# Attention tails packed into quarter and half arrays, and a ninth group of tokens by seven products

## The chip, the cores and the metric

The kernel runs on one core of a Trainium2 chip. A core has five engines with queues of their own: TensorE (PE in the profile), VectorE (DVE), ScalarE (ACT), GpSimd (POOL) and SyncE (SP). TensorE multiplies on an array of 128 rows by 128 columns and writes to eight PSUM banks; VectorE and ScalarE read these banks; GpSimd and SyncE here mostly start DMA transfers. The metric is the device time of one execution in microseconds (us), lower is better.

## What is computed

Attention with a bias by distance, for 8 batches, 8 heads, 576 positions and a head size of 64, followed by a feed-forward layer over the 4608 tokens. Cut to what matters:

```python
scores = scale * np.matmul(q, k.transpose(0, 1, 3, 2))       # [8, 8, 576, 576], scale = 1/8
bias = bias_table[bucket]                                    # bucket by |i - j|, 32 buckets
scores = scores + bias.transpose(2, 0, 1)[None]
attn = exp(scores - max);  attn = attn / (attn.sum(-1) + 1e-9)
x = np.matmul(attn, v)                                       # -> [4608, 512]
h = x @ w_in                                                 # [4608, 2048]
s = np.sin(alpha * h)
g = h + s * s / (alpha + 1e-09)
out = g @ w_out                                              # [4608, 512], float32
```

576 is 4 * 128 + 64: every batch has a last 64 keys and a last 64 queries that fill only half of an array. "Tails" below are these.

## The kernel before, in words

**Attention.** Heads go in four pairs p. A score tile (`qk_t`, task T) is 128 keys by 256 queries for both heads of a pair; the two heads of 64 dimensions lie in the upper and the lower 64 rows of the array ("rows" mode). Two such key chunks make one PSUM tile of 1024 columns, which ScalarE turns to `u` by one Exp (`exp_u`), and VectorE multiplies by exp(bias) where the bias is not constant (`band_t`). The tails have tasks of their own: L0 and L1 (`qk_tail`, last keys against the first 512 queries, two pairs each), R0 and R1 (`qk_r`, the first 512 keys against the last queries) and S (`qk_s`, last keys against last queries). For L and S the batches from the third on use `kd`, in which `corners` (VectorE) puts the last keys of both heads on a block diagonal: one matmul of the full array gives both heads. The first two batches use 64x64 tiles, one per head ("quad" mode).

**Values.** `av_w` (tasks av) multiplies `u` by v. It takes 128 queries as the stationary operand, and per pair it issues one matmul of 130 columns for the last keys and eight of 65 columns for the other keys (64 values and a column of ones for the sum). For w=0 it covers two chunks of 128 queries, for w=1 two chunks and the last 64 queries, which stand as a third chunk of 128 with the other half unused. `norm` (VectorE) divides, and `turn_x` (a DMA transpose, SP) or `turn_x_pe` (TensorE and a copy, batch 0) turns the result to `xT`. The tokens stand in the order of the output, 576 for each batch.

**Feed-forward.** The tokens go in blocks of 512, the last two of 448 and 576. For each block and each of 16 slices f of the hidden width, `moe_in` issues four matmuls against w_in, ScalarE does Sin (`moe_sin`), ScalarE or VectorE squares (`moe_sq`), VectorE forms g (`moe_g`). Groups of 512 tokens of g are multiplied by w_out. Groups 0 to 7 go by seven products of 256x256 blocks instead of eight (`moe_fast`, `products`): VectorE forms sums of g (`gate_sum`, four in two halves per group) and of w_out (`weight_sum`, once), and joins the products to quarters of the output (`quarter`, `quarter_sum`). Group 8 goes directly (`moe_out`, `moe_half`). Some products run as two at a time in halves of 64 rows ("rows" mode, listed in `OPT["rows"]`).

**The order.** `_graph` makes tasks with an engine, dependencies and rings of buffers; `_Plan.run` puts them in order; here the order of each engine is given outright by `LINE`. Each engine then works its queue strictly in that order. GpSimd's queue starts with `clear` (zeros in `us` and `kd`) and then issues the loads. `OPT["scalar"]` lists the tasks that ScalarE takes instead of VectorE.

The functions that the change touches, and what calls them:

Of the kernel before, what the change touches and what calls it, by code (L numbers as in the profile page):

```python
# [9 lines left out]
F16 = mybir.dt.float16  # L10
# [6 lines left out]
NP = H // 2  # L17
NF = FF // 128
XR = 4 * S
# [338 lines left out]
def _line(text):  # L358

    out, i = [], 0  # L360
    for x in text.split():
# [71 lines left out]


COLD = dict(turn_half=(0.22, 0.38), turn=(0.4, 0.48), qkT=(0.22, 0.42), qkR=(0.23, 0.43),
            qkL=(0.43, 0.62), qkS=(0.12, 0.24), turn_x=(0.2, 0.27))


def _graph(K, opt):
# [1265 lines left out]
```

## Time and profile before

| | before |
|---|---|
| median of 3 runs, us | 373.93 (372.23 to 373.96) |
| profiled execution, us from the first to the last instruction | 370.6 |
| TensorE matmul busy, us | 356.4 (96%), 4379 matmuls |
| VectorE busy, us | 318.8 (86%) |
| ScalarE busy, us | 318.4 (86%) |
| GpSimd busy, us | 87.9 (24%) |
| granted TensorE clock | 1.000 |

The page has no other time of the profiled execution than this span. A busy TensorE in the profile need not be at its peak: matmuls overlap, and one of 512 columns is shown with 379 ns, while four of them follow each other within 0.86 us. Where the rate matters, the view to read is the chain of work that ended last: each of its pieces shows how long a number of matmuls held the chain. An "idle before" that is named with an engine is time that the engine waited for it.

### The profile page before, as it was taken

How to read it: one execution, taken by the hardware profiler on the slowest of the kernel's cores; microseconds unless marked ns; L12 is line 12 of the kernel's file. 1: busy time of each engine (PE TensorE's matmuls, PEld its weight loads, DVE VectorE, ACT ScalarE, POOL GpSimd, SP SyncE). 2: the span in 40 equal slices, each digit the busy share in tenths (PEclk: the TensorE clock that was granted, in tenths of full speed). 3: DMA queues.
4: the chain of work that ended last, by engine and by line, in shares of the span. 5: the costliest groups of instructions: out<-in, count | busy, mean ns of one | idle time of the engine just before them, and what ended most of it. 6: DMA issues, size and time to landing. Idle time of an engine off the chain costs nothing.

```text
span 370.6 us, 10525 instructions
## 1 busy us (share of the span) xinstructions
PE 356.4 (96%) x4379; PEld 245.9 (66%) x4379; DVE 318.8 (86%) x711; ACT 318.4 (86%) x424; POOL 87.9 (24%) x105
## 2 busy tenths in 40 slices
PE   4969999999999999999999999999999999999996
PEld 3647546764666569755788987666965766745675
DVE  2679999999989998989998998899879997989733
ACT  5897999999999999999998999999899798476310
POOL 8895523085108000820050006200000000000000
PEclk9999999999999999999999999999999999999999
DMA  8999999899949954999799039907230012220014
GB/s 161 224 154 180 206 171 156 104 134 157 182 83 135 142 127 75 156 155 88 125 210 95 18 84 142 157 3 155 79 48 2 10 47 79 56 85 2 0 58 170
DMA packets 152415, 40.86 MB, mean 110 GB/s; under 512 B 134432, under 2 KB 151920, under 8 KB 152368
## 3 DMA queue, kind: packets, MB, share of 16 engines
q0 software_dynamic: 96656, 18.45, 60.2%
q1 hardware_dynamic: 55008, 21.22, 28.0%
q8 instruction: 34, 0.56, 0.6%
q10 hardware_dynamic: 704, 0.53, 0.6%
q14 instruction: 13, 0.11, 0.1%
HBM read 36.94 MB, written 15.93 MB: 143 GB/s over the span
## 4 chain that ended last, share of the span: by engine, by line
PE 87%; ACT 4%; POOL 3%; DMA 2%; DVE 2%; issue 1%; ACTq 0%; POOLq 0%; DVEq 0%
PE acc L1514 32%; PE acc L1611 26%; PE acc L1461 10%; PE acc L1405 9%; PE acc L1451 3%; PE acc L1558 3%; DMA wt<-in_k_dram 2%; PE acc L1364 2%; ACT s L1522 1%; PE acc L1395 1%; POOL mt L1292 1%; PE acc L1632 1%; DVE g L1543 1%; ACT u L1413 1%; POOL v L1219 1%
## 5 line engine op out<-in xcount | busy, mean ns | idle before, releaser
L1514 PE MATMUL acc<-xT,w_in 128*128 128x512 f16 (+3 forms) x704 | 134.2, 340 | 0.7 <-DVE g L1543 0.4
L1413 ACT ACTIVATE u<-acc 128x1024 f16<-128x1024 f32 x128 | 124.3, 1035 | 8.4 <-PE acc L1405 6.4
L1543 DVE SCALAR_TENSOR_TENSOR g<-s,inv_a,acc 128x512 f16<-128x512 f16 (+2 forms) x160 | 104.5, 691 | 8.6 <-ACT s L1527 6.5
L1522 ACT ACTIVATE s<-acc,alphaT 128x512 f16<-128x512 f32 (+2 forms) x144 | 93.2, 684 | 14.7 <-PE acc L1514 10.6
L1514 PEld LDWEIGHTS <-w_in 128*128 128x128 f16 x704 | 64.4, 98 | 55.8 <-DVE g L1543 1.8
L1611 PEld LDWEIGHTS <-g 128*128 128x128 f16 (+1 forms) x768 | 59.8, 96 | 18.0 <-issue 4.4
L1441 DVE TENSOR_TENSOR u<-u,toep 128x256 f16<-128x256 f16 (+1 forms) x128 | 59.4, 487 | 1.8 <-DMA toep<-e_sb 0.9
L1219 POOL DMA_DIRECT2D v<-in_v_dram x32 | 36.8, 1278 | 99.3 <-PE acc L1461 93.3
L1611 PE MATMUL acc<-w_out,g 128*128 128x256 f16 (+1 forms) x496 | 54.1, 271 | 0.0
L1405 PE MATMUL acc<-qT,kT 64*128 64x256 f16 x512 | 46.3, 279 | 3.9 <-DVE qT L1350 1.9
L1461 PE MATMUL acc<-v,u 128*128 128x65 f16 x1024 | 45.0, 193 | 0.1
L1527 ACT ACTIVATE s<-s 128x512 f16<-128x512 f16 (+2 forms) x67 | 41.4, 629 | 1.5
L1461 PEld LDWEIGHTS <-u 128*128 128x128 f16 x1024 | 40.6, 97 | 1.4 <-issue 0.5
L1611 PE MATMUL acc<-wt,g 128*128 128x256 f16 (+1 forms) x272 | 38.4, 272 | 0.0
L1611 PE MATMUL acc<-wt,sums 128*128 128x256 f16 (+1 forms) x272 | 34.6, 273 | 0.0
L1529 DVE TENSOR_TENSOR s<-s 128x512 f16<-128x512 f16 (+2 forms) x77 | 31.9, 422 | 2.6 <-ACT s L1522 2.3
L1472 DVE TENSOR_TENSOR xp<-acc,rden 128x256 f16<-128x256 f32 (+1 forms) x64 | 31.4, 491 | 2.2
L1405 PEld LDWEIGHTS <-kT 64*128 64x128 f16 x512 | 20.3, 96 | 16.1 <-issue 12.2
L1611 PEld LDWEIGHTS <-sums 128*128 128x128 f16 (+1 forms) x272 | 23.5, 97 | 7.9 <-issue 2.5
L1451 PE MATMUL acc<-vt,ut 128*128 128x130 f16 x128 | 28.3, 221 | 0.1
L1225 POOL DMA_DIRECT2D vt<-in_v_dram x16 | 14.1, 894 | 33.6 <-PE acc L1461 30.6
L1492 DVE COPY quarter<-acc 128x512 f32<-128x512 f32 x18 | 12.4, 687 | 9.3 <-PE acc L1611 4.7
(90 smaller groups left out, 361.6 us busy)
## 6 DMA issues: line engine op xcount, KB each, us to landing
out_dram<-quarter SPq DMA_DIRECT2D x32, 256.0 KB, 2.7
v<-in_v_dram POOLq DMA_DIRECT2D x32, 128.0 KB, 8.7
staged_k<-in_k_dram POOLq DMA_DIRECT2D x6, 576.0 KB, 10.8
staged_q<-in_q_dram POOLq DMA_DIRECT2D x5, 576.0 KB, 9.9
w_out<-in_moe_w_out_dram POOLq DMA_DIRECT2D x4, 512.0 KB, 8.7
w_in<-in_moe_w_in_dram POOLq DMA_DIRECT2D x4, 512.0 KB, 16.2
sums<-in_q_dram POOLq DMA_DIRECT2D x7, 144.0 KB, 5.6
out_dram<-outs SPq DMA_DIRECT2D x3, 256.0 KB, 2.0
```

The lines of the kernel that those rows point to most:

```text
L1219: self.nc.gpsimd.dma_start(out=self.vs[t % 2][:, c, :, 0:D], in_=src)
L1405: self.nc.tensor.matmul(out=s[:, o:o + 256], lhsT=self.kT[t % 2][r, p, 128 * c:128 * c + 128], rhs=self.qT[t % 2][r, p, 256 * w:256 * w + ...
L1413: self.nc.scalar.activation(out=c["u"], in_=c["s"], func=AF.Exp, scale=0.125)
L1441: self.nc.vector.tensor_tensor(out=io, in0=io, in1=m, op=ALU.mult)
L1451: nc.tensor.matmul(out=c["av"][:, 130 * j:130 * j + 130], lhsT=tail, rhs=vt[:, p, :], start=True, stop=True, skip_group_check=True)
L1461: nc.tensor.matmul(out=c["av"][:, 130 * j + 65 * a:130 * j + 65 * a + 65], lhsT=l, rhs=vv[:, ch, 2 * p + a, 0:65], start=False, stop=True, ...
L1514: self.nc.tensor.matmul(out=c["h"][:, x:y], lhsT=self.w_in[:, j, 128 * f:128 * f + 128], rhs=self.xT[:, j, at:at + y - x], start=(j == 0 a ...
L1522: self.nc.scalar.activation(out=c["s"], in_=c["h"], func=AF.Sin, scale=self.alphaT[:, f:f + 1])
L1527: self.nc.scalar.activation(out=c["s"], in_=c["s"], func=AF.Square)
L1529: self.nc.vector.tensor_tensor(out=c["s"], in0=c["s"], in1=c["s"], op=ALU.mult)
L1543: self.nc.vector.scalar_tensor_tensor(out=o, in0=c["s"][:, x:y], scalar=self.inv_a[:, f:f + 1], in1=c["h"][:, x:y], op0=ALU.mult, op1=ALU.add)
L1611: self.nc.tensor.matmul(out=c[to][:, 256 * k:256 * k + 256], lhsT=a[r, 128 * k:128 * k + 128], rhs=b[r, :], start=to not in c["began"], st ...
```

## The change

- **Last keys (L, S).** `kd` and `corners` go. `tail` issues four 64x64 matmuls for two pairs at once, into the four quarters of the array, in all batches. The heads that stand in the upper and lower half of the result alternate from pair to pair, and `mask`, `load_vt` (four smaller loads for each batch instead of two) and `memsets` follow that.
- **Last queries (values).** `av_w` covers two chunks for w=0 and w=1 alike. A new `av_tails` does the last queries of all four pairs in a batch: 64 queries are the stationary operand, and two pairs go to the two column halves of the array ("cols" mode). `norm_tails` and `turn_tails` (for batch 0 `turn_tails_pe`) bring them to a tile `xt`.
- **Groups.** A group is now the first 512 tokens of one batch, and the last 64 tokens of all eight batches are a ninth group. All nine blocks have 512 tokens and all nine groups go by seven products; the order of the groups is 0 to 6, the tails, 7. The last group ends by `ending`: its last product in two halves of 256 columns that are copied and stored one by one. `store` and its like write to the rows that belong to the group.
- **Start.** `clear` goes. The loads are in a new order.
- **Order and shares.** `LINE`, the products in rows mode, the list of ScalarE's tasks (51 squares instead of 67) and the number of `u` buffers (14 instead of 12) are new.

```diff
 LINE = """
-0 2 5 1 12 1 390 -21 229 -232 6 17 -112 324 -303 130 -137 154 134 17 -287 497 -265 268 -156 20 -37
...
+82 -68 66 8 2 -73 192 -125 43 7 3 -39 -12 18 20 -28 17 -35 112 -80 83 -99 -2 15 -6 102 -4 -36 42 -55
...
-    add("POOL", 2.05, E("clear"), seq="GQ")
...
-        T_v[t] += [gq(0.65, "load_vt", (t, a), deps=pre, pipe=0.27) for a in range(2)]
+        T_v[t] += [gq(0.6, "load_vt", (t, a, b), deps=pre, pipe=0.14) for a in range(2) for b in range(2)]
...
-            if not kind:
-                e = add("DVE", 0.42, E("corners", t, range(NP)), deps=[c], prio=0.3)
...
         ct = cells[t, ("L", p // 2)]
-        cr, cs = (cells[t, ("R", p // 2)], cells[t, ("S",)]) if w else (None, None)
-        need = tiles + [ct] + ([cr, cs] if w else [])
+        need = tiles + [ct]
...
+    def close_tails(t):
+
+        need = [cells[t, ("R", 0)], cells[t, ("R", 1)], cells[t, ("S",)]]
+        acell, xcell, users, xu = {}, {}, [], []
+        av = add("PE", 0.66, None, deps=[c["done"] for c in need] + T_v[t],
+                 prio=opt["p_av"], take=[(1, users)], mode="cols", name=f"avt{t}")
+        av.emit = lambda: K.av_tails(acell, tag(av), need[:2], t)
...
+            T_t[t] = add("SP", 1.2, lambda: K.turn_tails(xcell, t), deps=[nm], pipe=0.46,
+                         prio=0, pkt=15, flow=True, lat=0.8)
...
-        for t in range(t_lo, t_hi + 1):
+        t, at, to = GROUPS[lo // 512], lo % 512, (hi - 1) % 512 + 1
+        if t == T:
+            deps += T_t[at // 64:to // 64]
+        else:
             for x in T_x[t]:
...
-        (p4, p3), all_c = group((4, 3), (ww(3), s_of(4)), ([c22], [q22]), ())
-        c12[1].deps.extend(p3)
-        finish(21, p4, None, [])
+        if i < 8:
+            (p4, p3), all_c = group((4, 3), (ww(3), s_of(4)), ([c22], [q22]), ())
+            c12[1].deps.extend(p3)
+            finish(21, p4, None, [])
+        else:
+            all_c = ending(cell, i, ww(3), s_of(4), c22, q22, c12[1], xu)
...
+    def ending(cell, i, need4, need3, c22, q22, q12, xu):
+
+        p3 = [add("PE", 4 * 0.1092, E("products", cell, i, (3,), f, 0, False), prio=opt["p_mo"], mode="full",
+                  deps=need3(f) + [q22], name=f"mo{i}3.0.{f}") for f in range(0, NF // 2, 2)]
+        q12.deps.extend(p3)
+        every, ou = list(p3), []
+        for k in range(2):
+            p4 = [add("PE", 4 * 0.1092, E("products", cell, i, (4,), f, 0, False, (k,), 4), prio=opt["p_mo"],
+                      mode="full", deps=need4(f) + [c22], name=f"mo{i}4.{k}.{f}") for f in range(0, NF // 2, 4)]
...
-    line=_line(LINE), rows=((0,2), (3,2), (4,2), (5,0), (5,1), (5,2), (5,3), (6,0), (6,1), (8,2), (9,0), (9,1),
-    (10,2), (11,2), (11,3), (12,2), (12,3), (13,0), (13,2), (15,0), (15,1), (15,2), (16,3),
-    (18,2), (20,3)), strict=False,
...
-    blk=(512, 512, 512, 512, 512, 512, 512, 448, 576), fast=tuple(range(8)), split=True, no=2, nq=3, p_sum=0.1,
...
+    line=_line(LINE),
+    rows=((3, 0), (3, 1), (4, 0), (4, 1), (7, 0), (9, 0), (9, 1), (10, 0), (10, 1), (12, 0),
+        (12, 1), (16, 0), (16, 1), (18, 0), (18, 1), (19, 0), (19, 1)),
...
+    order={-1: _order("L0 L1 S R0 000 001 010 011 100 101 110 111 R1 200 201 210 211 300 301 310 311"),
+           0: _order("000 001 010 011 L0 100 101 110 111 L1 R0 200 201 210 211 R1 S 300 301 310 311")},
...
+    blk=(512, 512, 512, 512, 512, 512, 512, 512, 512),
+    groups=(0, 1, 2, 3, 4, 5, 6, 8, 7),
+    fast=(0, 1, 2, 3, 4, 5, 6, 7, 8),
...
-        kT, qT = self.kT[t % 2], self.qT[t % 2]
-        if t >= 2 and not (t == 2 and 0 in OPT["nat2"]):
-            self.nc.tensor.matmul(out=s[:, at:at + n], lhsT=self.kd[t % 2][:, p, :],
-                                  rhs=qT[:, p, q0:q0 + n], start=True, stop=True)
-            return
-        for a in range(2):
-            r = slice(64 * a, 64 * a + 64)
-            self.nc.tensor.matmul(out=s[r, at:at + n], lhsT=kT[r, p, 512:576],
-                                  rhs=qT[r, p, q0:q0 + n], start=True, stop=True)
...
+        for b in range(2):
+            for a in range(2):
+                r, o = slice(64 * a, 64 * a + 64), 64 * (a ^ b)
+                self.nc.tensor.matmul(out=s[o:o + 64, 512 * b + at:512 * b + at + n],
+                                      lhsT=kT[r, 2 * i + b, 512:576], rhs=qT[r, 2 * i + b, q0:q0 + n],
+                                      start=True, stop=True)
...
+    def av_tails(self, c, bank, rs, t):
+
+        nc = self.nc
+        c["av"] = self.acc[:, bank, 0:260]
+        vv, vt, us = self.vs[t % 2], self.vt[t % 2], self.us[t % 2]
+        for i in range(2):
+            for b in range(2):
+                p, r = 2 * i + b, slice(64 * b, 64 * b + 64)
+                nc.tensor.matmul(out=c["av"][r, 130 * i:130 * i + 130], lhsT=us[:, 64 * p:64 * p + 64],
+                                 rhs=vt[:, p, :], start=not i, stop=True, skip_group_check=True)
+            for a in range(2):
+                for ch in range(4):
+                    for b in range(2):
+                        o, r = 512 * a + 256 * b + 64 * ch, slice(64 * b, 64 * b + 64)
+                        at = 130 * i + 65 * a
+                        nc.tensor.matmul(out=c["av"][r, at:at + 65], lhsT=rs[i]["u"][:, o:o + 64],
+                                         rhs=vv[:, ch, 4 * i + 2 * b + a, 0:65],
+                                         start=False, stop=True, skip_group_check=True)
...
+    def turn_tails(self, xcell, t):
+        self.nc.sync.dma_start_transpose(out=self.xt[:, t, :].rearrange("d (c s) -> d c s", c=2),
+                                         in_=xcell["x"][:, :])
...
+        c["h"] = self.acc[:, bank, 0:n]
+        t, at = OPT["groups"][lo // 512], lo % 512
+        for j in range(4):
+            if t == T:
+                x = self.xt[:, at // 64:(at + n) // 64, 64 * j:64 * j + 64]
+            else:
+                x = self.xT[:, j, 512 * (t % 4) + at:512 * (t % 4) + at + n]
+            self.nc.tensor.matmul(out=c["h"], lhsT=self.w_in[:, j, 128 * f:128 * f + 128], rhs=x,
+                                  start=j == 0, stop=j == 3, skip_group_check=True)
```

More of the change, by code (lines that the diff above doesn't have):

```diff
@@ L18 @@
 NF = FF // 128
-XR = 4 * S
+XR = 4 * 512
 def _blocks(sizes):
@@ L454, in _graph @@
     T_q = [[None] * NP for _ in range(T)]
-    T_c = [[None] * NP for _ in range(T)]
+    T_t = [None] * T
     T_v = [None] * T
@@ L528, in _graph @@
     nat2 = opt["nat2"]
-    quad = lambda t: t < 2 or t == 2 and 0 in nat2
     staged = {}
@@ L707, in score @@
         else:
-            need = [x[p] for p in ps for x in (T_l, T_q[t])]
-            b = feed_one(c, 0.43, m, need, lambda s: K.qk_tail(s, t, i), 0.92, tr,
+            need = [x[t][p] for p in ps for x in (T_k, T_q)]
+            b = feed_one(c, 0.22, "quad", need, lambda s: K.qk_tail(s, t, i), 0.92, tr,
                      lambda: K.exp_u(c, "ut"), f"L{t}.{i}", [last_qk[t]], low=opt["low_t"])
@@ L736, in close @@
             T_x[t][p] = [x_dma(t, p, xcell, xu, norms)] * 2
+    def close_tails(t):
[4 more added lines that the diff above has]
+        av.emit = lambda: K.av_tails(acell, tag(av), need[:2], t)
+        for c in need:
+            c["users"].append(av)
+        last_av[t].append(av)
+        nm = add("DVE", 0.55, lambda: K.norm_tails(acell, xcell), deps=[av], prio=opt["p_norm"],
+                 take=[(xtr, xu)], name=f"nmt{t}")
+        users.append(nm)
+        if t in opt["xt_pe"]:
+            users, cell = [], {}
+            tr = add("PE", 0.13, None, deps=[nm], prio=opt["p_av"], take=[(1, users)],
+                     mode="full", name="turn_x")
+            tr.emit = lambda: K.turn_tails_pe(xcell, cell, tag(tr))
+            xu.append(tr)
+            T_t[t] = either(f"xt{t}", 0.25, 0.4, lambda act: K.copy_tails(cell, t, act), deps=[tr],
+                            prio=opt["p_norm"])
+            users.append(T_t[t])
+        else:
+            T_t[t] = add("SP", 1.2, lambda: K.turn_tails(xcell, t), deps=[nm], pipe=0.46,
+                         prio=0, pkt=15, flow=True, lat=0.8)
+            xu.append(T_t[t])
     def element(t):
@@ L748, in element @@
                     close(t, p, w, got)
+            if T_t[t] is None and all((t, x) in cells for x in (("R", 0), ("R", 1), ("S",))):
+                close_tails(t)
             yield
-        assert len(closed) == 2 * NP
+        assert len(closed) == 2 * NP and T_t[t] is not None
     BLK = _blocks(opt["blk"])
+    GROUPS = opt["groups"]
     NBLK = len(BLK)
@@ L1031, in _graph @@
     units(len(todo))
+    for i in range(2):
+        for m in over_nat[i]:
+            m.deps += nat_users[i]
     for t in plan.tasks:
@@ new lines @@
+    sq2.0 sq2.1 sq2.13 sq2.7 sq2.8 sq3.1 sq3.2 sq3.4 sq3.7 sq3.8 sq4.10 sq4.12 sq4.3 sq4.5
+    sq4.6 sq5.12 sq5.15 sq5.2 sq5.5 sq5.6 sq5.7 sq6.10 sq6.12 sq6.3 sq6.5 sq6.7 sq6.8 sq7.0
+    sq7.10 sq7.11 sq7.12 sq7.14 sq7.15 sq7.9 sq8.10 sq8.13 sq8.15 sq8.2 sq8.5 sq8.8 sq8.9
+    turn1.0.1 turn1.3.0 turn2.0.1 turn2.1.1 turn2.2.1 x0.0.0 x0.0.1""".split()),
+    nu=14,
+    nr=2,
+    nl=2,
+    ng=2,
+    win=7,
+    hold={(1, 0, 8): 0},
+    low=6,
+    low_t=6,
+    stick=0.0,
+    single=False,
@@ L1081 @@
+    p_in=0.8,
+    p_band=2.2,
+    p_norm=0.0,
+    p_sq=2.4,
+    p_g=0.2,
+    p_ev=0,
+    p_t1=(2.5, 2.5),
+    p_touch=-4,
+    late=0.0,
+    fills=FILLS,
+    warm=(),
+    low_clock=18.0,
+    nat2=(1,),
+    x_pe=((0, 0), (0, 1), (0, 2), (0, 3)),
+    xt_pe=(0,),
+    early=('T0.0.00', 'T0.0.01', 'T0.0.10', 'T0.0.11'),
+    gq="""n01 n02 n03 v0 b1 b3 i0 m0 i1 m1 m3 m2 i2 i3 n10 n11 o0 n12 o1 n13 o2 o3 v1 s20 n20 s21
+    n21 n22 n23 v2""".split(),)
 class _Ops:
@@ L1385, in qk_tail @@
     def qk_tail(self, s, t, i):
-        for p in range(2):
-            self.tail(s, 512 * p, 512, t, 2 * i + p, 0)
+        self.tail(s, 0, 512, t, i, 0)
     def qk_r(self, s, t, i):
@@ L1441, in band_t, with av_w @@
         self.nc.vector.tensor_tensor(out=io, in0=io, in1=m, op=ALU.mult)
-    def av_w(self, c, bank, tiles, cr, ct, t, p, w):
+    def av_w(self, c, bank, tiles, ct, t, p, w):
         nc = self.nc
-        n = 3 if w else 2
-        c["av"] = self.acc[:, bank, 0:130 * n]
+        c["av"] = self.acc[:, bank, 0:260]
         vv, vt = self.vs[t % 2], self.vt[t % 2]
-        for j in range(n):
+        for j in range(2):
             o = 512 * (p % 2) + 256 * w + 128 * j
-            tail = ct["u"][:, o:o + 128] if j < 2 else self.us[t % 2][:, 64 * p:64 * p + 128]
-            nc.tensor.matmul(out=c["av"][:, 130 * j:130 * j + 130], lhsT=tail, rhs=vt[:, p, :],
-                             start=True, stop=True, skip_group_check=True)
+            nc.tensor.matmul(out=c["av"][:, 130 * j:130 * j + 130], lhsT=ct["u"][:, o:o + 128],
+                             rhs=vt[:, p, :], start=True, stop=True, skip_group_check=True)
@@ new lines, in turn_tails, with turn_tails_pe @@
+    def turn_tails(self, xcell, t):
+        self.nc.sync.dma_start_transpose(out=self.xt[:, t, :].rearrange("d (c s) -> d c s", c=2),
+                                         in_=xcell["x"][:, :])
+    def turn_tails_pe(self, xcell, cell, bank):
+        cell["o"] = o = self.acc[:, bank, :].bitcast(F16)
+        for i in range(2):
+            self.nc.tensor.transpose(out=o[:, 128 * i:128 * i + 128],
+                                     in_=xcell["x"][:, 128 * i:128 * i + 128], identity=self.ident[:, :])
@@ L1482, in turn_x_pe, with copy_tails @@
+    def copy_tails(self, cell, t, act):
+        self.copy(self.xt[:, t, :], cell["o"][:, 0:256], act)
     def turn_x_pe(self, xcell, cell, w, bank):
         cell["o"] = o = self.acc[:, bank, :].bitcast(F16)
-        for i in range(3 if w else 2):
-            self.nc.tensor.transpose(out=o[:, 128 * i:128 * i + 128], in_=xcell["x"][:, 2 * w + i, :],
+        for i in range(2):
+            at = 256 * w + 128 * i
+            self.nc.tensor.transpose(out=o[:, 128 * i:128 * i + 128], in_=xcell["x"][:, at:at + 128],
@@ L1592, with products @@
     HOME = {1: "X", 6: "X", 7: "X", 4: "X", 2: "Y", 5: "Z", 3: "Z"}
-    def products(self, c, i, names, f0, turn, rows):
+    def products(self, c, i, names, f0, turn, rows, ks=range(2), n=2):
         g, s, w, t = self.g[i], self.sums[:, i % 2], self.w_out, self.wt
-        for f in range(f0, f0 + 2):
+        for f in range(f0, f0 + n):
             u = f + NF // 2
@@ L1604, in products @@
                   3: (g[:, u, 0:256], w[:, u, 256:512])}
-            for k in range(2):
+            for k in ks:
                 for x, n in enumerate(names):
```

241 lines of the change are left out of this document (115 added, 126 removed), and 123 rows, old and new, of the table LINE.

## The prediction

> **What bounds the kernel now.** I read the page's head first, then the busy time by stages, then the chain of waits.
>
> ```profile
> PE 356.4 (96%) x4379; PEld 245.9 (66%) x4379; DVE 318.8 (86%) x711; ACT 318.4 (86%) x424; POOL 87.9 (24%) x105
> ...
> 0.00:30.00 30.00, 20.20 (x365) 14.23 (x366) 17.75 (x49) 23.89 (x32) 26.74 (x48) 1.00 1.22 177
> 30.00:42.80 12.80, 12.31 (x263) 8.97 (x260) 12.33 (x37) 12.10 (x14) 7.77 (x9) 1.00 1.23 197
> 42.80:350.00 307.20, 306.38 (x3622) 209.40 (x3621) 281.91 (x617) 280.32 (x377) 53.36 (x49) 1.00 0.89 101
> 350.00:370.60 20.60, 17.46 (x139) 13.30 (x136) 6.80 (x12) 2.04 (x4) 0.00 (x0) 1.00 0.30 103
> ```
>
> The columns after the stretch are its length, then TensorE matmul, weight load, VectorE, ScalarE and GpSimd busy. From 42.8 to 350 us TensorE is busy 306.4 of 307.2 us, while VectorE and ScalarE stand at 92% and 91%. So each us of TensorE work taken out of this stage shortens the span, until VectorE or ScalarE fills up. Before 42.8 us TensorE waits: its busy shares there are made of short overlapping matmuls, and GpSimd (26.7 of 30 us) and ScalarE (23.9) are the full engines.
>
> The chain gives rates:
>
> ```profile
> 52.61 0.87 PE acc L1611 x8
> 53.48 4.32 PE acc L1514 x20
> 58.35 1.42 PE acc L1611 x12
> 61.08 0.68 PE acc L1369 x12
> 140.51 0.32 PE acc L1405 x4
> 141.28 0.22 PE acc L1405 x4
> 146.08 0.06 PE acc L1451
> 146.14 0.24 PE acc L1461 x8
> 152.95 0.98 PE acc L1364 x8
> ```
>
> L1514 x20 in 4.32 us is 0.216 us for 512 columns; L1611 x8 in 0.87 is 0.109 for 256. A group of values is 0.06 + 0.24 = 0.30 us (L1451 of 130 columns, eight L1461 of 65). A switch of mode costs about 0.10: L1405 x4 takes 0.32 us beside full-array work and 0.22 between two rows pieces; L1611 x12 takes 1.42 instead of 1.31.
>
> **The change part by part.**
>
> *Last queries (values).* Before, they are a third chunk for each pair:
>
> ```profile
> L1451 PE MATMUL acc<-vt,us 128*128 128x130 f16 x32 | 7.0, 219 | 0.0
> 17.60 0.45 PE L1340 MATMUL acc<-ident,wt 96*64 96x96 f16 x12
> 19.43 0.70 PE L1340 MATMUL acc<-ident,wt 96*64 96x96 f16 x24
> 23.03 0.31 PE L1369 MATMUL acc<-qT,kT 64*64 64x64 f16 x8
> L1369 PE MATMUL acc<-qT,kT 64*64 64x64 f16 x16 | 0.6, 198 | 0.0
> ```
>
> 32 groups of 0.30 are 9.6 us, 1.2 for each batch. After, each of two column halves gets two matmuls of 130 columns (0.06) and sixteen of 65. Column halves do run beside each other: 12 more transposes (L1340) take 0.70 - 0.45 = 0.25 us, 21 ns each, 42 for each half, and they have 96 columns. The nearest row for a short matmul with a weight load of 64 columns is L1369: eight in 0.31 us, the last one 0.198 long, so four per tile with a pitch of 0.112/3 = 37 ns. The batch costs 0.12 + 16 * 0.037 = 0.71, bounds 0.60 (30 ns, L1461's own pitch) and 0.79 (42 ns). Gain 0.49 * 8 = 3.9 us, ends 3.3 and 4.8.
>
> The Trainium skill, "TensorE: Matmul & The Clock Gate", section "LDWEIGHTS (loading the stationary operand)", gives the load time as columns divided by 1.2, which is 53 ns for 64 columns, and "TensorEngine Tiling (Array Packing)", section "Restrictions", says that column tiling disables the fast weight load; this speaks against the change. By it a batch would cost 2 * 9 * 0.053 = 0.96 and the gain would be an estimated 1.9 us. The trace does not agree: both rows above hold loads of 64 columns and stay at 37 and 42 ns.
>
> *Last keys (L, S).* L1364 x8 in 0.98 holds four of 512 and four of 64 columns. 16 tasks L cost 4 * 0.216 per batch, in full as in quad mode. Four tiles side by side need half: 0.43 * 8 = 3.5 us gained. The trace shows two tiles side by side, not four (61.08: four of 512 and eight of 64 columns in 0.68 with a switch), so the other end is 0. I take 3.5, since both kinds of halves, rows and columns, run in parallel in it. S: about 0.3 gained.
>
> *Ninth group.*
>
> ```profile
> L1558 PE MATMUL acc<-w_out,g 128*128 128x512 f16 x48 | 13.5, 379 | 0.0
> L1632 PE MATMUL acc<-w_out,g 128*128 128x256 f16 x32 | 4.5, 273 | 0.0
> L1578 DVE TENSOR_TENSOR sums<-sums,g 128x1024 f16<-128x1024 f16 x16 | 10.8, 682 | 0.0
> L1622 DVE TENSOR_TENSOR quarter<-quarter,acc 128x512 f32<-128x512 f32 x24 | 16.4, 685 | 4.4 <-PE acc L1611 2.8 <-ACT quarter L1490 1.4
> L1543 DVE SCALAR_TENSOR_TENSOR g<-s,inv_a,acc 128x512 f16<-128x512 f16 x128 | 91.0, 744 | 3.5 <-ACT s L1527 2.5
> L1543 DVE SCALAR_TENSOR_TENSOR g<-s,inv_a,acc 128x448 f16<-128x448 f16 x16 | 10.6, 678 | 3.5 <-ACT s L1527 3.4
> L1543 DVE SCALAR_TENSOR_TENSOR g<-s,inv_a,acc 128x64 f16<-128x64 f16 x16 | 4.5, 279 | 1.6 <-ACT s L1527 0.6
> L1254 DVE TENSOR_TENSOR kd<-kT 64x256 f16<-64x256 f16 x12 | 3.4, 284 | 0.4 <-DMA kT<-staged_k 0.3
> L1529 DVE TENSOR_TENSOR s<-s 128x512 f16<-128x512 f16 x58 | 23.9, 421 | 2.3 <-ACT s L1522 2.0
> L1527 ACT ACTIVATE s<-s 128x512 f16<-128x512 f16 x54 | 33.4, 632 | 1.1
> ```
>
> 48 * 0.216 + 32 * 0.109 = 13.9 us become 7 * 16 * 0.109 = 12.2: 1.7 gained. Splitting of blocks (64-column pieces) and two transposes of batch 0 that fall away: 0.2. VectorE gets 8 sums (5.5 us) and 3 quarter sums (2.1), loses `corners` (3.4) and one of two pieces of g in the old last block (106.1 - 144 * 0.711 = 3.7), and takes 16 squares from ScalarE (+6.7; ScalarE -10). Together about 318.8 + 7.2 = 326; ScalarE about 308. Neither is on the path if TensorE stays the full engine. In the last 20 us VectorE was busy 6.8, which covers the sums of the last group; their delay is covered by its first two products (3.5 us).
>
> *Switches.* L and S in quad and the new values in cols are separate pieces where the batches from the third on had full-array work: four pieces per batch. If each stands alone it costs two switches: 6 * 4 * 0.20 + 2 * 0.20 = 5.2 us. Against it, rows chunks of products that count go from 9 to 17; each that joins two rows pieces saves two switches: 8 * 0.2 = 1.6. Bounds +5.2 and -1.6; I take +2.5, as L0, L1 and S follow each other in the list.
>
> *Queues.* SP gets 28 transposes of 512 instead of 640 tokens and seven small ones, GpSimd two more loads per batch (16 * 0.65 = 10 us). After 42.8 us GpSimd is busy 53 of 307, so this costs nothing; the cover would be gone only in the first 30 us, where one batch's two more loads (1.3 us) stand against `clear`.
>
> *First block.*
>
> ```profile
> 0.74 0.36 POOL L1209 MEMSET us<- 128x320 f16 x1 [0.29 <-POOLq L1689]
> 2.28 0.77 POOL L1213 DMA_DIRECT2D sums<-in_k_dram  x1
> 26.65 1.49 POOL L1235 DMA_DIRECT2D w_out<-in_moe_w_out_dram  x2
> 28.12 0.76 POOL L1230 DMA_DIRECT2D w_in<-in_moe_w_in_dram  x1
> 34.17 0.75 POOL L1230 DMA_DIRECT2D w_in<-in_moe_w_in_dram  x1 [1.75 <-DMA w_out<-in_moe_w_out_dram]
> DMA to landing us min/median/max: 11.2/16.2/17.4
> 42.84 0.39 PE L1514 MATMUL acc<-xT,w_in 128*128 128x512 f16 x1
> L1405 PE MATMUL acc<-qT,kT 64*128 64x256 f16 x52 | 4.6, 272 | 0.3 <-ACT u L1413 0.2
> L1461 PE MATMUL acc<-v,u 128*128 128x65 f16 x89 | 4.2, 193 | 0.1
> ```
>
> `clear` held GpSimd's first load back by 1.54 us. The first w_in was issued at 28.12 and needs 11 to 17 us to land, 39 to 45, beside a first feed-forward matmul at 42.84; two w_out loads stand directly ahead of it. The last two rows are groups of the stretch from 30 to 42.8 us: at the rates above, 52 of L1405 (two at a time) are 2.8 us and 89 of L1461 are 2.7; with the smaller groups of that view TensorE did 9.3 us of work there, so 3.5 us were lost, and more before. If the loads move and block 0 no longer waits for R and S, TensorE fills some 7 us sooner, at about 36; of these 7 us about 2.5 were lost. Ends: 0, and 5 if it fills at 30. I take 2.5.
>
> *Sum.* 370.6 - 3.9 - 3.5 - 0.3 - 1.7 - 0.2 + 2.5 - 2.5 = 361.0 us span. The median of the runs stands 3.3 us above the profiled span (373.93 to 370.6); with the same, 364.3 us, that is 2.6% faster.
>
> **The rivals.**
>
> *Tiles share the array only two at a time.* Four 64x64 tiles gain nothing over two, and L keeps its time: 3.5 + 0.3 us back, 368.1. For it: no row shows four. Against it: both kinds of halves run in parallel.
>
> *Weight loads pace the column halves.* The transposes load 96 rows of weights, the new values 128. If the 42 ns are the load's and go with its rows, the pitch is 42 * 128 / 96 = 56 ns, the batch costs 0.12 + 16 * 0.056 = 1.02 and the gain is 0.18 * 8 = 1.4: 366.8. For it: 42 ns fits a load as well as 96 columns. Against it: 64 rows of load in L1369 took 37, not 28. The Trainium skill's "TensorE: Matmul & The Clock Gate", in the section named above, would give about the same time by its 53 ns, though by columns and not by rows.
>
> *VectorE becomes the bound (the other side).* Its queue is in order; before, it stood idle 370.6 - 318.8 = 51.8 us, of which 25.3 in the full stage, where its waits for ScalarE and TensorE sit. If the new order leaves it this idle time, the span is 326 + 51.8 = 377.8 and the time 381. It decides from an idle time of 46.5 us on (326 + 46.5 + 3.3 = 375.8). Against it: VectorE had waits because TensorE was full. In a span of 361 us it needs (326 - 17.8 until 30 us - some 5.8 until 36 - 6.8 at the end) / 305 = 97% of the full stage, which is tight, but a stretch of before holds that on all three engines:
>
> ```profile
> 80.00:100.00 20.00, 20.00 (x165) 11.42 (x164) 19.63 (x43) 19.70 (x30) 10.14 (x10) 1.00 2.06 161
> ```
>
> *The tails' group comes late.* Block 7 needs the last queries of all eight batches, with a DMA transpose of 2.9 us at the end:
>
> ```profile
> xT<-xp SPq DMA_TRANSPOSE x28, 2.9
> ```
>
> If nothing covers it, TensorE waits for S or R, the values (0.7), the division (0.6) and 2.9, some 5 us: 369.3. Against it: R1 stands ahead of half of the batch's T tasks in the list.
>
> *Much sooner start and few switches.* Start at its end (2.5 more) and switches at -1.6 (4.1 more): 357.7.
>
> **How the numbers follow.** A measurement of this kernel can tell about 0.5% from no change (1.9 us). Chances: the sum as forecast, 359.5 to 367, 0.50; two at a time 0.13; loads that pace 0.07; tails late 0.08; much sooner 0.10; VectorE bound 0.12 (372.5 to 385). Faster by over 0.5% (below 372.06): all but the last, 0.88, less 0.03 for a tail that is later than 5 us, 0.85; slower (above 375.8): most of VectorE's case, 0.10; between, 0.05. The range 357 to 371 leaves out VectorE's case and part of the soonest. The forecast's own range is 359.5 to 367.
>
> **What would show it.** Last keys: four matmuls of 512 columns on 64*64 tiles hold the chain for 0.22 us and not 0.43. Last queries: 36 matmuls of a batch in 0.6 to 0.8 us. First L1514-like matmul near 36 us, with w_in issued ahead of w_out. The full stage shows TensorE still at 99% with VectorE near 97%; no direct 512-column products against w_out; the time from the last input matmul to the end is at least 12 us. Wrong if VectorE, not TensorE, has no gaps between start and end, if TensorE waits for `xt`, or if pieces of 0.1 us around quad and cols groups sum to over 5 us.

## The result, and the profile after

| | before | after |
|---|---|---|
| median, us | 373.94 (372.23 to 374.29) | 382.86 (381.46 to 384.27) |
| profiled execution, us from the first to the last instruction | 370.6 | 381.2 |
| TensorE matmul busy, us | 356.4 | 358.3 |
| VectorE, ScalarE busy, us | 318.8, 318.4 | 324.7, 305.3 |
| mean granted TensorE clock | 1.000 | 0.964 |

The ratio is 1.0246, with a 95% interval of 1.0207 to 1.0285: the changed kernel is about 2.5% slower, where 2.6% faster was forecast. The 370.6 us are a quick execution of the kernel before: of 18 timed later, the four at a mean clock of 1.000 spanned 370.2 to 371.0 us and the other fourteen, at 0.985 to 0.995, 371.0 to 373.1. The span grew by 10.6 us, and the same stretches as before show in which part (columns: length, then TensorE matmul, weight load, VectorE, ScalarE and GpSimd busy, granted clock, DMA share, GB/s):

```profile
0.00:30.00 30.00, 21.31 (x337) 14.85 (x339) 19.46 (x56) 19.42 (x24) 24.14 (x43) 0.79 1.18 171
30.00:38.94 8.94, 8.94 (x247) 7.45 (x241) 7.64 (x29) 7.51 (x11) 4.40 (x8) 0.94 1.22 196
38.94:350.00 311.06, 308.54 (x3762) 204.08 (x3758) 286.23 (x635) 276.78 (x369) 66.41 (x67) 1.00 0.88 101
350.00:360.00 10.00, 6.84 (x58) 5.70 (x57) 6.36 (x12) 0.60 (x2) 0.00 (x0) 0.94 0.13 45
360.00:381.20 21.20, 12.66 (x71) 8.90 (x69) 5.06 (x9) 0.98 (x2) 0.00 (x0) 0.71 0.27 78
```

The middle is nearly as full as before (308.5 of 311.1 us). The first feed-forward matmul starts at 38.94 instead of 42.84 us, but the clock in the first 30 us is 0.79. After 350 us the kernel needs 31.2 us instead of 20.6, TensorE is idle for 11.7 of them, and the clock falls to 0.71. The waits of this last stretch, from 348 us on (engine, result and line that waited, what it waited for, sum, times, longest):

```profile
ACT quarter L1585 <- DMA out_dram<-quarter: 16.4, 1, 16.4
...
PE acc L1698 <- ACT quarter L1585: 4.1, 1, 4.1
DVE quarter L1587 <- DMA out_dram<-quarter: 3.9, 2, 3.6
...
PE acc L1698 <- DVE g L1630: 3.2, 1, 3.2
```

ScalarE stands idle for 16.4 us before a copy into a quarter buffer, and what ended that idle time is a store that landed; the products before it on TensorE had ended 3.4 us earlier. TensorE then waits 4.1 us in all for that copy. The chain of work (start, length, what) says it in order:

```profile
348.91 7.17 DMA out_dram<-quarter
...
356.20 0.69 DVE quarter L1587
356.89 0.67 DVE g L1630
...
357.58 0.69 DVE sums L1665
...
359.47 7.46 DMA out_dram<-quarter
...
367.04 0.61 ACT quarter L1585
...
367.69 3.59 PE acc L1698 x16
...
372.10 5.51 PE acc L1698 x32
```

Stores hold the chain for 7.17 and 7.46 us, each time with the stores that are queued ahead. VectorE's queue is in order: until 356.20 it waits for a free quarter buffer (3.6 us), and behind that copy stand `g` and `sums` of the last group, so TensorE waits too (3.2 us for `g`). The 32 matmuls of 256 columns at the end take 5.51 us instead of 32 * 0.109 = 3.5: behind these gaps the granted clock is 0.60 from 367 to 378 us. The DMA rows of 349 to 358 us (busy share of 16 engines in tenths, rate, and the issues with their size) show the store itself:

```profile
DMA  0010111112011111111111111111111111111111
GB/s 0 5 32 18 36 46 18 41 27 32 14 36 55 46 46 55 46 46 46 55 46 46 55 46 46 55 46 46 46 55 46 46 55 46 46 55 46 46 46 55
...
q1 hardware_dynamic: 369, 0.37, 12.8%
...
out_dram<-quarter SPq DMA_DIRECT2D x3, 128.0 KB
```

A share of 12.8% is that of 2 of 16 engines (12.5%). In these 9 us they moved 0.37 MB, 41 GB/s, so that a store of 128 KB takes about 3 us and the eight of the tails' group (1 MB) some 25 us, from 348 us to 373. `put` writes each of them with one transfer over [2 batches, 64 rows, 256 columns]. The Trainium skill, "DMA: Bandwidth & Descriptors", section "Why a DMA increments its semaphore by 16 and not by 1", says that a transfer is spread over the largest number of engines up to 16 that divides the size of the slowest dimension of both of its patterns; for this pattern that is 2, and the trace agrees.

### The profile page after: what moved, and what is told of

Read it like the earlier page. It is cut to its first block, busy times and chain, and to the rows that moved or that the text cites. A ratio compares the mean times of both kernels' runs of the same rounds, so it can differ in the third digit from the quotient of the medians.

```text
span 381.2 us, 10669 instructions
## 1 busy us (share of the span) xinstructions
PE 358.3 (94%) x4457; PEld 241.0 (63%) x4457; DVE 324.7 (85%) x737; ACT 305.3 (80%) x406; POOL 94.9 (25%) x117
## 4 chain that ended last, share of the span: by engine, by line
PE 37%; DMA 6%; DVE 4%; ACT 2%; issue 1%; SPq 0%; DVEq 0%; ACTq 0%
PE acc L1698 14%; PE acc L1604 14%; DMA out_dram<-quarter 4%; PE acc L1469 3%; PE acc L1518 3%; DVE g L1630 2%; DMA xT<-xp 2%; PE acc L1513 1%; ACT s L1609 1%; DVE s L1616 1%; DVE quarter L1587 0%; PE acc L1459 0%; DVE quarter L1709 0%; ACT L1477 0%; SPq L1739 0%
## 5 line engine op out<-in xcount | busy, mean ns | idle before, releaser
L1604 PE MATMUL acc<-xT,w_in 128*128 128x512 f16 x512 | 115.3, 379 | 1.4 <-DMA w_in<-in_moe_w_in_dram 0.8
L1609 ACT ACTIVATE s<-acc,alphaT 128x512 f16<-128x512 f32 x144 | 92.6, 685 | 18.2 <-PE acc L1604 14.5
L1630 DVE SCALAR_TENSOR_TENSOR g<-s,inv_a,acc 128x512 f16<-128x512 f16 x144 | 102.3, 744 | 3.4 <-ACT s L1614 2.2
L1604 PEld LDWEIGHTS <-w_in 128*128 128x128 f16 x576 | 55.6, 98 | 62.7 <-issue 1.8
L1505 DVE TENSOR_TENSOR u<-u,toep 128x1024 f16<-128x1024 f16 (+1 forms) x128 | 57.8, 485 | 0.5 <-ACT u L1477 0.3
L1698 PE MATMUL acc<-wt,g 128*128 128x256 f16 x288 | 40.6, 285 | 4.9 <-ACT quarter L1585 4.1
L1616 DVE TENSOR_TENSOR s<-s 128x512 f16<-128x512 f16 x93 | 37.9, 421 | 6.5 <-ACT s L1609 6.1
L1698 PE MATMUL acc<-wt,sums 64*128 64x256 f16 (+1 forms) x432 | 40.4, 276 | 0.0
L1301 POOL DMA_DIRECT2D vt<-in_v_dram x32 | 27.7, 1011 | 23.8 <-PE acc L1538 18.8
L1587 DVE COPY quarter<-acc 128x512 f32<-128x512 f32 (+1 forms) x21 | 14.2, 675 | 22.1 <-PE acc L1698 14.6
L1614 ACT ACTIVATE s<-s 128x512 f16<-128x512 f16 x51 | 31.8, 629 | 0.8
L1585 ACT ACTIVATE quarter<-acc 128x512 f32<-128x512 f32 (+1 forms) x16 | 9.3, 580 | 27.6 <-DMA out_dram<-quarter 16.4
L1698 PEld LDWEIGHTS <-sums 64*128 64x128 f16 (+1 forms) x432 | 27.5, 97 | 5.9 <-issue 1.7
L1545 DVE TENSOR_TENSOR xp<-acc,rden 128x256 f16<-128x256 f32 x64 | 27.2, 425 | 2.3
```

What stands on the lines that cost most here:

```text
L1301: self.nc.gpsimd.dma_start(out=dst[:, :, b, at:at + 64], in_=src)
L1505: self.nc.vector.tensor_tensor(out=io, in0=io, in1=m, op=ALU.mult)
L1604: self.nc.tensor.matmul(out=c["h"], lhsT=self.w_in[:, j, 128 * f:128 * f + 128], rhs=x, start=j == 0, stop=j == 3, skip_group_check=True)
L1609: self.nc.scalar.activation(out=c["s"], in_=c["h"], func=AF.Sin, scale=self.alphaT[:, f:f + 1])
L1614: self.nc.scalar.activation(out=c["s"], in_=c["s"], func=AF.Square)
L1616: self.nc.vector.tensor_tensor(out=c["s"], in0=c["s"], in1=c["s"], op=ALU.mult)
```

## The experiments

**Two stores instead of one.** The suspected transfer alone is changed: one for each batch, 64 rows each.

```diff
-            rows = self.out.rearrange("(t s) n -> t s n", s=S)[2 * (tau % 4):2 * (tau % 4) + 2, 512:S, at:at + n]
+            for b in range(2):
+                r = S * (2 * (tau % 4) + b) + 512
+                self.nc.sync.dma_start(out=self.out[r:r + 64, at:at + n], in_=o[64 * b:64 * b + 64])
+            return
```

> The stores of the tails' group go out as two transfers of 64 rows each instead of one over two batches; all else is the changed kernel. Theory A (a transfer whose outermost dimension is 2 is spread over 2 of the 16 DMA engines, takes about 3.5 us of its queue for 128 KB, the quarters' ring of three runs full and the products behind it wait): the 7 us gaps at 349 and 359 us go, the DMA share in a tail store is no longer 0.12, and the time falls by 13 to 17 us to 366 to 370 us. Theory B (the rows are slow because they lie 576 KB apart in memory, not because of the shape): the stores stay slow, the time stays at 381 to 384. Theory C (VectorE is the bound, as one rival of the prediction had it): the time falls by less than 3 us, and VectorE has no gaps at the end.

Measured: 372.06 us (370.54 to 373.17), ratio to before 0.9952 (0.9932 to 0.9973). The edit is worth 10.8 us. The same DMA rows of this kernel, and its last two stretches:

```profile
DMA  7508418319139157067000000000850841922929
...
q1 hardware_dynamic: 959, 0.80, 40.2%
...
out_dram<-quarter SPq DMA_DIRECT2D x12, 64.0 KB, 2.1
```

```profile
350.00:360.00 10.00, 8.63 (x80) 7.58 (x78) 7.74 (x13) 0.60 (x1) 0.00 (x0) 1.00 0.44 104
360.00:369.00 9.00, 4.52 (x40) 3.65 (x38) 2.49 (x4) 0.38 (x1) 0.00 (x0) 1.00 0.32 100
```

Twelve stores of 64 KB are issued in the time of three of 128 KB; the median one lands in 2.1 us, the clock stays at 1.00 and the end takes 19.0 us instead of 31.2. Theory A holds, though the gain ends 2 us short of its range. Theory B falls, since every row still lies where it lay (the batches are 576 rows of 2 KB apart, which is 1152 KB and not 576), and so does theory C. Nothing else was changed, so the way in which the tails' group is stored is shown as the cause of the loss.

**Two transfers of the slow shape.** Was it the shape, or that a single large transfer was under way at a time?

```diff
-            rows = self.out.rearrange("(t s) n -> t s n", s=S)[2 * (tau % 4):2 * (tau % 4) + 2, 512:S, at:at + n]
+            rows = self.out.rearrange("(t s) n -> t s n", s=S)[2 * (tau % 4):2 * (tau % 4) + 2, 512:S]
+            for h in (0, n // 2):
+                self.nc.sync.dma_start(out=rows[:, :, at + h:at + h + n // 2], in_=o[:, h:h + n // 2])
+            return
```

> The changed kernel (382.86 us), whose stores of the tails' group are again two transfers for each 128x256 block, but split by columns: each still goes over [2 batches, 64 rows] and takes 128 of the 256 columns. Theory A (the outermost dimension of two is what leaves a transfer on 2 of 16 DMA engines): the share stays at 0.12 to 0.13 while they drain, at 48 GB/s or less, and the time stays at 381 to 385 us (more if rows of 512 bytes go slower than rows of 1 KB). Theory B (one large transfer at a time is what is slow, and two run beside each other, as in the kernel with two stores): the time falls below 376 and the share rises to 0.25 or more.

Measured: 383.99 us (382.32 to 385.9), ratio 1.0268 (1.0246 to 1.0291). DMA rows of 349 to 360 us:

```profile
DMA  1111111111111111111111111111111111111111
...
q1 hardware_dynamic: 915, 0.46, 14.2%
...
out_dram<-quarter SPq DMA_DIRECT2D x8, 64.0 KB
```

As many transfers of 64 KB in all as in the kernel with two stores, and still the share of about 2 of 16 engines. Theory B falls: the outermost dimension decides, not the size or the number of the transfers. The rows here are 512 bytes long where the kernel with two stores has 1 KB, but the changed kernel's single store, with rows of 1 KB, had the same rate (42 GB/s in both views).

**The slow store with a deeper ring.** Four quarter buffers instead of three (`nq=4`; to make room `a16` moves to an unused part of `sums`).

```diff
-    nq=3,
+    nq=4,
```

> The changed kernel (382.86 us) with its single store for two batches, and four quarter buffers. Theory A (a store at 3.5 us for each 128 KB is itself the bound of the end: six of 128x512 for the tails and then the last group's stand in one queue): a fourth buffer lets the products of one more quarter run ahead, but the stores still end no sooner; the time falls by 0 to 3.5 us, to 379.5 to 383. Theory B (the depth of the ring is what costs, and the transfer itself would be hidden with one more buffer): the time falls by more than 7 us, to below 376.

Measured: 379.32 us (377.96 to 381.72), ratio 1.0137 (1.0106 to 1.0167): 3.5 us less than 382.86, 0.2 us beyond the range of theory A and far from theory B. A fourth buffer delays the wait and does not remove it: ScalarE still stands idle 11.0 us before a copy until a store lands. That profile is of the slowest of the four executions.

**The deeper ring with two stores.** The same edit on the kernel with two stores.

> The kernel with two stores, with four quarter buffers in the ring instead of three. Theory A (the waits that are left at the end, such as the copy into a quarter at 358.31 us, are for a free quarter): the wait of the copies for a store is gone and the time falls by 1 to 2 us to 370 to 371. Theory B (that copy waits for the last group's hidden values to be summed on VectorE, and the ring is free by then): no change, 372 within 0.7 us.

Measured: 370.5 us (369.97 to 371.2), ratio 0.9913 (0.9896 to 0.9931), against 0.9952 (0.9932 to 0.9973) with three buffers. The gain is about 1.5 us, but the intervals almost touch, and the two were timed beside different runs of the kernel before. The traces show half of it: TensorE's busy time from 350 to 360 us goes from 8.63 to 9.31, and its wait for the copy that the theories name from 1.4 to 0.7 us. With three buffers this copy starts at 358.31 us, 0.7 us after the product that it copies; with four it starts as the product ends (358.02 and 358.00). That points to the buffer, as theory A has it, though the profile names VectorE and no store as what ended the wait.

**The first loads sooner.** In the kernel with two stores TensorE starts at 6.21 us, when `ident` lands. The first loads are put in another order:

```diff
+    ahead = [7, 4, 0, 1, 2, 5, 3, 8]
+    order = sorted([t for t in order if t.idx in ahead], key=lambda t: ahead.index(t.idx)) \
+        + [t for t in order if t.idx not in ahead]
```

> The kernel with two stores (372.06 us, span 369.0), with the first loads in the order: SyncE tab, k, k, alpha; ScalarE ident, q, cst, q. Theory A (the late first loads hold back the first products, and with them the whole stage until the first feed-forward block): first matmul at about 5 us instead of 6.21, first exponential at 9 to 10 us instead of 11.59, first feed-forward matmul 1 to 2.5 us before 38.47, time 369.5 to 371. Theory B (the first block is set by GpSimd's queue and the landing of its weights, whatever the first loads do): first exponential sooner, but the first feed-forward matmul stays at 38.5 within 0.5 us and the time at 372 within 0.7 us.

Measured: 371.1 us (370.65 to 371.86), ratio 0.993 (0.9912 to 0.9948), which isn't told apart from 0.9952; the time lies between the ranges of the two theories. The first matmul moves to 4.90 us, and the first feed-forward matmul stays (39.0 us, before 38.5), so theory A falls.

**Loads and ring together.**

> Two stores, first loads in the new order, and four quarter buffers together. If both of the single edits gain (1 to 2.5 us and 1 to 2 us), they add up, since one acts before 40 us and the other after 350: 367.5 to 370. If neither does: 372 within 0.7 us.

Measured: 370.26 us (368.55 to 370.89), ratio 0.9901 (0.9879 to 0.9924): what the ring gives, and nothing on top. This and the one with the ring alone are the fastest versions found, 1% ahead of the kernel before. The runs with fills and with the last queries twice start from this one.

**A full clock at the start.** From about 17 to 30.6 us TensorE runs at half its clock here, much as in the changed kernel. Sixteen pieces of 256 columns on constants, which nobody reads, are put into its gaps; in the trace they are 18 matmuls between 15.0 and 18.8 us, since a piece in column halves is two:

```diff
-FILLS = ()
+FILLS = ((17, 3), (18, 3), (19, 3), (20, 3), (21, 2), (23, 2))
```

> The kernel with two stores, first loads in the new order and four quarter buffers (370.26 us), with 16 matmuls of 256 columns on constants, whose results nobody reads, in TensorE's gaps between 14 and 21 us. Theory A (TensorE's clock falls to half from 17.4 to 31 us because of these gaps, and the half clock is what holds back the first block): the granted clock from 18 to 30 us is 0.9 or more, the first feed-forward matmul starts 1 to 3 us sooner and the time is 367.5 to 369.5. Theory B (ScalarE and GpSimd set the pace of the first 30 us, so that TensorE would only wait instead of going slowly): with the clock at 0.9 or more no change, 370.3 within 0.7 us, and TensorE's busy time from 18 to 30 us falls below 10 of 12 us. If the clock stays at half, the run tells nothing between them.

Measured: 371.48 us (368.75 to 372.14), ratio 0.9926 (0.9899 to 0.9952); no gain. The stretches without the fills:

```profile
12.00:18.00 6.00, 4.66 (x77) 2.93 (x75) 4.33 (x10) 6.00 (x7) 5.16 (x9) 0.91 1.37 232
18.00:30.00 12.00, 11.88 (x193) 8.02 (x194) 10.40 (x23) 9.97 (x13) 11.53 (x20) 0.50 1.33 148
```

and with them:

```profile
12.00:18.00 6.00, 5.76 (x89) 3.52 (x91) 4.26 (x10) 6.00 (x8) 5.51 (x9) 1.00 1.33 218
18.00:30.00 12.00, 9.93 (x250) 7.31 (x246) 10.66 (x25) 12.00 (x15) 11.10 (x20) 1.00 1.40 164
```

and, of the same kernel, the row of TensorE's waits between 44 and 345 us for transposed tokens:

```profile
PE acc L1604 <- DMA xT<-xp: 2.7, 5, 1.2
```

At the full clock TensorE waits instead of going slowly, and ScalarE, busy 12.00 of 12.00 us, is the full engine of that stretch. The first block starts at 36.7 instead of 38.3 us, yet the span is 369.1 against 369.0. The last row shows one place where the gain went back: TensorE waits 2.7 us for transposed tokens, where it waited 1.4 without the fills. Theory B holds, though the time ends 0.5 us above its range.

**Many fills.** The list has 47 of them (one more than the expectation counts), 66 matmuls between 13.1 and 23.4 us in the trace.

```diff
-FILLS = ()
+FILLS = ((13, 2), (14, 2), (16, 2), (17, 4), (18, 4), (19, 4), (20, 4), (21, 4), (22, 3), (23, 3), (24, 3), (26, 3), (27, 3), (28, 3), (29, 3))
```

> As the run with 16 of these matmuls, with 46 of them from 12 to 24 us. Theory A: the clock is full from 18 to 30 us even if the fewer do not suffice; what the fills take from TensorE (46 * 0.107 = 4.9 us, of which about half falls into its gaps) is less than the half clock costs, and the time is 368 to 370. Theory B: the time is 370.3 to 372.5 at a full clock.

Measured: 372.05 us (370.45 to 374.49), ratio 0.996 (0.9936 to 0.9983), at a full clock: theory B, 1.8 us more than without fills. The first block starts only at 41.2 us, 2.9 later than without fills, and the span is 1.3 us longer (370.3 to 369.0). So in neither direction does the time follow the start of the first block one to one.

**The order written out by hand.** The kernel with two stores, placed by the planner alone.

```diff
-    line=_line(LINE),
+    line=(),
```

> The kernel with two stores (372.06 us), without the order written out by hand: the planner places every step as soon as it can. Theory A (the written order holds TensorE back before 38.5 us, since it places steps after loads that land late): the first feed-forward matmul 1 us or more sooner and the time 369 to 371. Theory B (TensorE loses some 17 us before the first block in any order, and what an order decides is how many switches and waits the middle has): the time rises by 1 to 8 us, to 373 to 380.

Measured: 452.08 us (446.89 to 454.61), ratio 1.205 (1.1992 to 1.2108). Both theories missed this by far. TensorE is busy 268.1 of 310 us between 40 and 350 us, and its longest sum of waits is `PE acc L1604 <- DMA xT<-xp`, 20.4 us in eight waits. It tells nothing of the start, since everything else moved too. What it tells is that transposed tokens that come in time are a part of what the written order does: with it, TensorE waited 0.6 us for them in the middle.

**Last keys twice.** The four matmuls of `qk_tail` are issued a second time, in the kernel with two stores.

```diff
+        self.tail(s, 0, 512, t, i, 0)
```

> As the run before it in this list, but each task L issues its four 64x64 matmuls of 512 columns twice (the second set writes the same values again). If four tiles run side by side, 16 further sets of 0.22 us cost at most 3.5 us on TensorE; if only two at a time, 6.9 us. If TensorE is no longer the bound in the full stage, less than 2 us.

Measured: 373.42 us (371.28 to 374.94) against 372.06 in the same set, 1.4 us more, with ratios whose intervals overlap (0.9963 to 1.0012 and 0.9932 to 0.9973). The time alone decides little: it speaks against 6.9 us, but it also lies under the 2 us of the third case, a TensorE that is no longer the bound. The timeline decides:

```profile
111.75 0.69 PE L1432 MATMUL acc<-qT,kT 64*64 64x512 f16 x16
112.37 1.05 PE L1699 MATMUL acc<-wt,sums 64*128 64x256 f16 x16
```

A piece with eight matmuls of 512 columns and eight of 64 holds TensorE for 0.62 us, up to the next row. With four of 512 it takes 0.40 us in the changed kernel (the row at 228.12 us below). So four more cost 0.22 us, and two at a time would have cost 0.43: four do run beside each other. Why the time grew by less than 16 * 0.22 = 3.5 us is not shown.

**Last queries twice.** All matmuls of `av_tails` are made twice; numerator and denominator double.

```diff
-        for i in range(2):
+        for i, rep in ((0, 0), (0, 1), (1, 0), (1, 1)):
...
-                                 rhs=vt[:, p, :], start=not i, stop=True, skip_group_check=True)
+                                 rhs=vt[:, p, :], start=not i and not rep, stop=True, skip_group_check=True)
```

> The kernel with two stores, first loads in the new order and four quarter buffers (370.26 us), with every matmul of the last queries' values (36 for each batch, in column halves) made twice, so that numerator and denominator double and their ratio stays. Theory A (the halves run beside each other at 30 ns for each tile, as the trace of the changed kernel shows): 8 * 0.62 = 5.0 us more if all of it is on the path, 3 to 5 us in fact: 373 to 375.5. Theory B (loads of 64 columns pace them at 53 ns for each tile): 8 * 2 * 9 * 0.053 = 7.6 us more, 376.5 to 378.

Measured: 379.67 us (377.19 to 382.1), ratio 1.0158 (1.0117 to 1.02), 9.4 us more: over both theories. The time alone would speak against 30 ns for each tile, but the timeline (start, length, engine, line, operation, idle before) doesn't:

```profile
41.89 0.32 PE L1459 MATMUL acc<-qT,kT 64*128 64x64 f16 x5 [3.34 <-issue]
...
80.53 0.25 PE L1531 MATMUL acc<-vt,us 128*64 128x130 f16 x2
80.61 0.42 PE L1538 MATMUL acc<-v,ur 128*64 128x65 f16 x16
80.87 0.22 PE L1531 MATMUL acc<-vt,us 128*64 128x130 f16 x2
...
81.89 0.41 PE L1459 MATMUL acc<-qT,kT 64*128 64x64 f16 x16
```

Four rounds of 18 matmuls take 1.36 us up to the next piece, with the switch behind them; the two rounds of the changed kernel take 0.74. So the doubling itself is 0.62 us for each batch, 5.0 in all, as theory A has it. The other 4.4 us are not explained. In the profiled execution, the slowest of the four (span 380.3 us, the others 375.4 to 378.5), the first row shows a large piece: TensorE stands still for 3.34 us in the middle of a group, with no wait that the profile names. Why is open, and so is whether the other executions have it; in this stretch, from 36 to 43 us, all 16 DMA engines are full, and one packet of the instruction queue is among their work, so a late load of instructions is a guess.

## Why the prediction was wrong

**The step that failed: queues.** It counted SP's transposes and GpSimd's loads and concluded "this costs nothing". The stores of the new group, which stand in SP's queue as well, have no term in it, though `put` was in the diff. In the kernel before, four stores of 256 KB at the end landed in 2.2 us each. Leaving the new ones out amounts to taking a store of half the size to do no worse; it took about 3 us. Eight of them are due at the end, the ring of three quarters fills, and the end of the kernel, where nothing is left to cover it, pays 10.8 us. A bound from the nearest row would have been of no help, as that row was a store of another shape: what was missing was the shape.

**The term that was mis-sized: first block, -2.5 us.** The block does come 3.9 us sooner, and next to nothing is gained. The step took 9.3 us of work out of 12.8 and called 3.5 lost. It left out the switches of mode that it priced at 0.10 us two paragraphs above: in the trace, 24 of them lie in that stretch. With 2.3 us for these, 1.2 us were lost there, and 17.5 before 30 us. Counted the same way over the matmuls of the trace (0.42 ns for a column, 2.6 ns for a matmul, divided by the tiles that run beside each other, 0.097 us for a switch), TensorE loses 18.8 us before its first block in the kernel before and 18.4 in the one with two stores: -0.4 instead of -2.5. The runs with other loads and with a full clock leave the time where it was, and the one with many fills lengthens it.

**What was right.** By the same count TensorE's work falls from 331.3 to 321.5 us, 9.8 less where the terms summed to 9.6, and the switches go from 157 to 187, +2.9 where 2.5 was taken. The chain of the changed kernel shows two of the terms:

```profile
228.12 0.40 PE acc L1432 x12
...
229.68 0.25 PE acc L1538 x15
...
229.99 0.25 PE acc L1538 x14
```

- *Last keys:* twelve matmuls of `tail` (four of 512 columns at once, 0.22 us; eight of 64, 0.06; a switch, 0.10) hold the chain for 0.40 us, about the sum; the -3.5 us stand, and the rival with two tiles at a time falls.
- *Last queries:* a round of one group of two pairs takes 0.31 us, a batch 0.62, where 0.71 was taken and 0.60 to 0.79 were the bounds; the gain is 8 * (1.2 - 0.62) = 4.6 us instead of 3.9. The rival with loads that pace the halves falls: 16 matmuls on two halves with a load of 64 columns each take 0.25 us, about 30 ns for each matmul of a half. The 53 ns for such a load by the Trainium skill's "TensorE: Matmul & The Clock Gate", section "LDWEIGHTS (loading the stationary operand)", do not agree with that.
- *VectorE as the bound:* 324.7 us of work as estimated (326), but TensorE is the engine without gaps (308.5 of 311.1 us against VectorE's 286.2). The other side came true by another mechanism than the rival's.
- *Tails late:* in the middle TensorE waits 0.4 us for transposed tokens in the changed kernel and for none of the tails, so this rival did not happen.

**What was missing in the sum.** Without the slow store the kernel is 1.6 us of span ahead of before (369.0 to 370.6), not 9.6. The work and the switches give -6.9. To that come -0.4 before the first block, +2.7 of small losses in the middle (2.1 to 4.8 us by the same count) and +3.0 at the end. There the ninth group's products, sums and copies follow each other, and the prediction had its "first two products" cover them all; 2.2 us of it are two waits of TensorE for copies (1.4 and 0.8), of which the deeper ring takes 0.7 away. Where the losses of the middle lie is known for a part only: the waits that the profile names there are some 1.2 us in the kernel with two stores and 0.6 in the one before. The step from span to time, +3.3 us, was too large as well: the profile before was of a quick execution, and the changed kernel's time stands 1.7 us above its profiled span (382.86 to 381.2).

## What to carry to other kernels

For every store or load that a change adds, write down its access pattern and look at its outermost dimension: a transfer of 128 KB over two batches ran on 2 of 16 DMA engines, one after another at about 3 us each; transfers of 64 rows and 64 KB landed in 2.1 us and side by side. Here these transfers stood at the end of the kernel, where the ring of output buffers handed their delay to ScalarE, VectorE and TensorE in turn; whether they would have been hidden earlier was not tried. And before calling idle time "lost", take everything off it that has a price already: with two stores the first block came 4.4 us sooner (38.5 to 42.8 us), and that took only 0.4 us off TensorE's lost time.

## What the hardware showed

- A transfer whose outermost dimension is 2 used 12.8 to 14.2% of the 16 DMA engines at 41 to 42 GB/s, whether it moved 128 or 64 KB; transfers of 64 rows and 64 KB took shares of up to 0.9.
- In the kernel with two stores, new loads and four quarters TensorE's clock fell to half at about 17 us although no gap of 0.6 us or more stood in the 4 us before, and it stayed at half while TensorE was busy 11.88 of 12 us. Sixteen pieces of matmuls in these gaps kept it at 1.00: the mean clock was 0.995 to 1.000 in seven executions with them and 0.981 to 0.986 in six without. The kernel before ran at 1.000 in some executions and at 0.985 to 0.995 in most. Which measure of activity decides it was not tried.
- Four 64x64 tiles, and two 128x64 column halves, run beside each other: 0.22 us for four of 512 columns, 30 ns for each tile of 65 columns. By the count above, a switch between full, rows, cols and quad mode costs 0.09 to 0.15 us.
